# Turned weights at four places modulo 512, and four sequences of the six terms of h

## Chip, cores and metric

The kernel runs on one core of one Trainium2 chip. The metric is the device time of one execution in microseconds. Before the change three runs gave 657.39 us as their median (657.28 to 657.51).

## What is computed

Two attention steps and a gated feed-forward layer, in float32:

```python
p_packed = sm_attn(p, k, v)                 # 32 packed rows per head
out = sm_attn(q, p_packed, p_packed)        # batch 8, heads 8, 576 tokens, 64 wide
x = out.transpose(0, 2, 1, 3).reshape(4608, 512)
h = x @ w_in                                # 512 -> 2048
g = h * sigmoid(1.702 * h)
return g @ w_out                            # 2048 -> 512
```

## The kernel before, in words

The 2048 inner columns are walked in two phases (`ph` 0 and 1), and in each phase in four units `u` of two chunks of 128 columns. A pair of chunks with its rows of `w_out` has the number kp = 4 ph + u; "the four inner chunks" of the change are the four u. For each batch b (0 to 7) and each half (288 of 576 tokens) a unit does this:

- `h_mm` (line 714, matmul at L725) makes h for the unit's two chunks. The second attention step is folded in: the stationary operand is a 128x128 piece of `m` (the packed values times w_in), the moving operand is a row of `a` (the attention weights), 288 columns. Both are split into an upper and a lower float32r part, so that one chunk takes six matmuls into one bank: (even/odd head `eo`, part of m, part of a) = term 0 (0, upper, upper), 1 (0, lower, upper), 2 (1, upper, upper), 3 (1, lower, upper), 4 (0, upper, lower), 5 (1, upper, lower). All units take them in the order 0 to 5. There are 16 halves x 16 chunks x 6 = 1536 of them.
- ScalarE applies the gate (`g_main` L745, `g_over` L751), VectorE forms seven sums of quarters (`g_sum` L795), and both split them into upper and lower parts (`g_upper`, L126; `g_lower` L815): the tile `gs`.
- `prod` (L902) multiplies by w_out after Strassen's scheme with seven products (the "turned weights": sums and differences of quarters of w_out, upper and lower parts, in the tiles `Wa` with four blocks and `Wb` with three). Each product takes three matmuls, upper x upper, upper x lower, lower x upper: stationary a 128x128 piece of `gs`, moving 256 columns of `Wa` or `Wb`. There are 128 unit-halves (2 phases x 16 halves x 4 units); 116 go this way, and 16 more that gather the tokens left over by each half (tiles named `over`): 132 x 7 products x 3 = 2772 matmuls. The other 12 unit-halves, of batch 0, use `prod0` (L842): 12 matmuls each of 512 columns.

Four accumulator banks A to D and two pairs of banks for h hold the results. `a_lower` (L691, VectorE) writes the lower part of `a` for a half, `m_lower` (L597, VectorE) that of `m` for two units; `a_upper` is a copy (L126 on ScalarE, or L128 on VectorE).

The order of all work on every engine is written out by hand, as a list of some thousand steps at the end of the kernel, and each engine runs its own in that order; waits are set by what an instruction reads and writes. A wait stands on the first matmul that reads the late operand, and all later matmuls stand behind it, since TensorE runs them in order.

SBUF places: `places` (line 81) reserves all tiles once, in the order of the table, each slot rounded up to 32 bytes per partition. Tiles `a`, `m` and `gs` stand before the part that the change touches and start at 192 modulo 512 bytes. The weights Wa0 to Wb3 stand behind five small tags (mx1, nb1, sm1, again, mx2), which take 448 bytes together, so that all eight start at 128 modulo 512; their blocks are 1024 bytes long, so every moving operand of `prod` starts at 128 modulo 512. Every stationary operand of `prod` and of `h_mm` starts at 192. The moving operands of h start at 192 (terms 0 and 1), 320 (2 and 3), 448 (4) and 64 (5).

Of the kernel before, what the change touches and what calls it, by code (L numbers as in the profile page):

```python
# [21 lines left out]
def kernel(  # L22
# [41 lines left out]
    G = S // NPK  # L64
    FC = 512
    HC = FC // 2
# [17 lines left out]
        ("a", 2 * S, ABUFS), ("aT", KC * 2 * P, 1), ("X", 8 * P, XBUFS), ("r", 7 * HC, 2),  # L84
        ("pn", 2 * D, 1), ("PT", P, 8), ("raw", 2 * FC, RBUFS), ("over0", 2 * NM, 1),
        ("over1", 2 * NM, 1), ("over2", 2 * NM, 1), ("over3", 2 * NM, 1), ("mx1", 2, 2),
        ("nb1", 2, 2), ("sm1", 2, 2), ("again", 1, 2), ("mx2", G, 2), ("Wa0", 8 * HC, 1),
        ("Wb0", 6 * HC, 1), ("Wa1", 8 * HC, 1), ("Wb1", 6 * HC, 1), ("Wa2", 8 * HC, 1),
        ("Wb2", 6 * HC, 1), ("Wa3", 8 * HC, 1), ("Wb3", 6 * HC, 1), ("rs1", 1, 4), ("rsa", 1, 2),
        ("sm2", G, 2), ("rs2", G, 2),  # L90
    )
    for tag, words, bufs in places:
        for i in range(bufs):
# [24 lines left out]
    def pair_bank(name):  # L118
        return ps_h.tile([P, 2, FC], F32, tag="psh", name=name)
# [588 lines left out]
    def over_tile(ph, g, u):  # L708
        if (ph, g, u) not in over_g:
            over_g[ph, g, u] = wk.tile([P, 2, NM], F32, tag=f"over{u}", name=f"over_{ph}_{g}_{u}")  # L710
        return over_g[ph, g, u]

    def h_mm(ph, b, half, u, i, ap_=None):
        if i == 0 and not ap_:
            st["h", ph, b, half, u] = pair_bank(f"h_{ph}_{b}_{half}_{u}")
        h = st["h", ph, b, half, u][:, i, :NH]
        f = 2 * NU * ph + 2 * u + i
        m, a = st["m", b, f // CF], st["a", ph, b, half]
        at = slice(f % CF * P, (f % CF + 1) * P)
        terms = [(eo, part, 0) for eo in range(2) for part in range(2)]  # L720
        terms += [(eo, 0, 1) for eo in range(2)]
        for n, (eo, part, ap) in enumerate(terms):
            if ap_ not in (None, ap):
                continue
            nc.tensor.matmul(  # L725
                h, m[:, part, eo, at], a[:, ap, eo * NH : (eo + 1) * NH],
                start=(n == 0), stop=(n == len(terms) - 1), skip_group_check=ap_ is not None,
            )
# [229 lines left out]
    def store(b, half, r=None, block=None, engine=nc.sync):  # L958
# [43 lines left out]
        (a_lower_copy, 0, 0, 0, 0), (warm, 7, 1, "D"), (a_lower_mm, 0, 0, 0, 1),  # L1002
        (begin_w, "out", 2, 0, None), (load_w, "in", 0, 1, 1), (max2, 0, 1),
        (h_mm, 0, 0, 0, 0, 0, 0), (a_lower_copy, 0, 0, 0, 1), (load_w, "in", 0, 2, 1),
        (wa_upper, 0, 2, 4), (h_mm, 0, 0, 0, 0, 1, 0), (join_w, "out", 2, 0, None),
        (begin_w, "out", 3, 0, None), (wa_lower_mm, 0, 1), (load_w, "in", 1, 0, None), (sub2, 0, 1),
        (begin_w, "in", 0, 0, 1), (join_w, "out", 3, 0, None), (h_mm, 0, 0, 0, 0, 0, 1),
        (exp2, 0, 1), (table, "gelu"), (h_mm, 0, 0, 0, 0, 1, 1), (join_w, "in", 0, 0, 1),
        (wa_lower_mm, 0, 0), (load_w, "in", 1, 1, None), (g_main, 0, 0, 0, 0, 0), (sum2, 0, 1),
# [830 lines left out]
```

## Time and profile before

| what | value |
|---|---|
| median of three runs | 657.39 us |
| the profiled execution, its own time | 657.49 us |
| span of its instructions | 655.7 us |
| TensorE matmul busy | 647.9 us, 99% of the span |
| VectorE busy | 558.0 us, 85% |
| ScalarE busy | 410.4 us, 63% |
| mean granted TensorE clock | 1.000 |

The span runs from the first to the last instruction; 1.8 us of the execution lie around it. Matmuls are pipelined: one is shown as lasting some 280 to 295 ns while the next starts 113 to 134 ns after it, so busy time says little about how fast they follow each other. That is read from the chain of waits: a piece of it gives the time from the start of a run of matmuls to the start of what follows, and its count; the quotient is the spacing.

### The profile page before, as it was taken

How to read it: one execution, taken by the hardware profiler on the slowest of the kernel's cores; microseconds unless marked ns; L12 is line 12 of the kernel's file. 1: busy time of each engine (PE TensorE's matmuls, PEld its weight loads, DVE VectorE, ACT ScalarE, POOL GpSimd, SP SyncE). 2: the span in 40 equal slices, each digit the busy share in tenths (PEclk: the TensorE clock that was granted, in tenths of full speed). 3: DMA queues.
4: the chain of work that ended last, by engine and by line, in shares of the span. 5: the costliest groups of instructions: out<-in, count | busy, mean ns of one | idle time of the engine just before them, and what ended most of it. 6: DMA issues, size and time to landing. Idle time of an engine off the chain costs nothing.

```text
span 655.7 us, 15348 instructions
## 1 busy us (share of the span) xinstructions
PE 647.9 (99%) x6263; PEld 593.7 (91%) x6263; DVE 558.0 (85%) x1151; ACT 410.4 (63%) x772; POOL 5.4 (1%) x15
## 2 busy tenths in 40 slices
PE   7999999999999999999999999999999999999997
PEld 5777898989989899898999799999999999999997
DVE  3978989789898997978898787977889887978897
ACT  5976977778685886966768755444444463444441
POOL 1100000000000000000000000000000000000000
PEclk9999999999999999999999999999999999999999
DMA  9866565673856737465476341333232423332342
GB/s 336 298 220 236 187 165 204 174 279 73 227 208 162 267 56 298 172 166 178 150 261 186 124 179 65 111 89 121 82 116 88 127 88 89 107 103 75 90 133 109
DMA packets 59318, 104.92 MB, mean 160 GB/s; under 512 B 31408, under 2 KB 36272, under 8 KB 58352
## 3 DMA queue, kind: packets, MB, share of 16 engines
q1 hardware_dynamic: 59104, 103.81, 48.5%
q8 instruction: 49, 0.80, 0.5%
q14 instruction: 21, 0.17, 0.1%
q10 hardware_dynamic: 144, 0.13, 0.1%
HBM read 70.51 MB, written 33.42 MB: 159 GB/s over the span
## 4 chain that ended last, share of the span: by engine, by line
PE 94%; DMA 3%; ACT 1%; SPq 1%; DVE 0%; issue 0%; ACTq 0%
PE h L725 30%; PE accC L902 13%; PE accB L902 13%; PE accA L902 13%; PE accD L902 6%; PE psm_None L573 4%; PE accB L842 2%; PE accB_over L902 2%; PE accA_over L902 2%; PE accC_over L902 2%; PE accA L842 2%; DMA home_m<-w_in 1%; DMA home<-w_in 1%; PE ps L617 1%; PE accD L521 1%; PE ps L310 1%
## 5 line engine op out<-in xcount | busy, mean ns | idle before, releaser
L725 PE MATMUL h<-a,m 128*128 128x288 f32 x1536 | 226.2, 294 | 0.0
L725 PEld LDWEIGHTS h<-a,m 128*128 128x128 f32 x1536 | 208.8, 188 | 2.0 <-ACT gs L126 0.8
L815 DVE TENSOR_TENSOR gs<-X,gs 128x896 fp32r<-128x896 f32 x116 | 125.2, 1087 | 29.8 <-ACT gs L126 29.2
L126 ACT CAST gs<-X 128x896 fp32r<-128x896 f32 (+2 forms) x118 | 106.4, 909 | 62.7 <-DVE X L795 46.1
L795 DVE TENSOR_TENSOR X<-X 128x256 f32<-128x256 f32 (+1 forms) x348 | 108.5, 331 | 20.8 <-ACT X L745 17.3
L745 ACT ACTIVATE X<-h 128x512 f32<-128x512 f32 (+1 forms) x129 | 76.3, 595 | 70.3 <-PE h L725 33.2
L902 PE MATMUL accC<-Wa,gs 128*128 128x256 f32 x696 | 98.4, 281 | 0.0
L902 PE MATMUL accB<-Wb,gs 128*128 128x256 f32 x696 | 97.7, 281 | 0.0
L902 PEld LDWEIGHTS accB<-Wb,gs 128*128 128x128 f32 x696 | 88.3, 189 | 6.0 <-issue 3.4
L902 PEld LDWEIGHTS accC<-Wa,gs 128*128 128x128 f32 x696 | 88.6, 189 | 5.4 <-issue 4.7
L902 PE MATMUL accA<-Wa,gs 128*128 128x256 f32 x348 | 60.3, 282 | 0.0
L902 PE MATMUL accA<-Wb,gs 128*128 128x256 f32 x348 | 59.3, 279 | 0.0
L902 PE MATMUL accD<-Wa,gs 128*128 128x256 f32 x348 | 57.2, 281 | 0.0
L751 ACT ACTIVATE over<-h 128x64 f32<-128x64 f32 x128 | 35.2, 287 | 32.5 <-PE h L725 32.2
L902 PEld LDWEIGHTS accA<-Wa,gs 128*128 128x128 f32 x348 | 49.4, 189 | 2.4 <-issue 2.1
L902 PEld LDWEIGHTS accD<-Wa,gs 128*128 128x128 f32 x348 | 48.1, 189 | 2.6 <-issue 2.6
L902 PEld LDWEIGHTS accA<-Wb,gs 128*128 128x128 f32 x348 | 48.9, 189 | 0.0
L597 DVE TENSOR_TENSOR m<-psm_None,m 128x1024 fp32r<-128x1024 f32 x31 | 37.7, 1217 | 2.2 <-ACT m L126 2.2
L126 ACT CAST m<-psm_None 128x1024 fp32r<-128x1024 f32 x31 | 30.8, 1016 | 10.2 <-PE psm_None L573 10.0
L573 PE MATMUL psm_None<-w_in,PT 64*32 64x512 f32 x496 | 32.2, 596 | 0.1
L691 DVE TENSOR_TENSOR a<-xt,a 128x576 fp32r<-128x576 f32 x31 | 23.2, 749 | 3.2 <-ACT a L126 3.1
L126 ACT CAST a<-xt 128x576 fp32r<-128x576 f32 (+1 forms) x30 | 19.7, 660 | 5.2 <-DVE xt L671 5.2
(208 smaller groups left out, 774.6 us busy)
## 6 DMA issues: line engine op xcount, KB each, us to landing
part<-r SPq DMA_DIRECT2D x14, 896.0 KB, 6.8
p<-part SPq DMA_DIRECT2D x14, 896.0 KB, 5.4
q<-q SPq DMA_DIRECT2D x16, 576.0 KB, 6.1
o<-r SPq DMA_DIRECT2D x16, 512.0 KB, 6.3
raw_out_None<-w_out SPq DMA_DIRECT2D x16, 511.8 KB, 4.0
v<-v SPq DMA_DIRECT2D x7, 1024.0 KB, 6.7
raw_in_None<-w_in SPq DMA_DIRECT2D x12, 511.8 KB, 5.6
k<-pk SPq DMA_DIRECT2D x8, 640.0 KB, 3.9
```

The source lines that it names most:

```text
L126: nc.scalar.copy(dst, src)
L310: nc.tensor.matmul(bank[32 * j : 32 * j + 32, :NH], kq["p", b][rows(eo), j, :], kq["k", b][rows(eo), half, j, :], start=True, stop=True,)
L573: nc.tensor.matmul(banks[eo][32 * j : 32 * j + 32], PT[rows(eo), j, :], w_in_sb[c % 2][rows(eo), j, at], start=True, stop=True,)
L597: nc.vector.tensor_tensor(m[:, 1, :, at], st["bank", "m", b, c, part], m[:, 0, :, at].bitcast(F32), op=ALU.subtract,)
L691: engine.tensor_tensor(even_odd(a[:, 1], eo), even_odd(st["t", 2, b, half], eo), even_odd(a[:, 0], eo).bitcast(F32), op=ALU.subtract,)
L725: nc.tensor.matmul(h, m[:, part, eo, at], a[:, ap, eo * NH : (eo + 1) * NH], start=(n == 0), stop=(n == len(terms) - 1), skip_group_check= ...
L745: nc.scalar.activation(X[:, :4].rearrange("p (f t) n -> p f (t n)", f=2)[:, chunks(f)], st["h", *k][:, chunks(f), :NM], AF.Gelu_apprx_sigm ...
L751: nc.scalar.activation(over_part(ph, b, half, u), st["h", ph, b, half, u][:, :, NM:NH], AF.Gelu_apprx_sigmoid, scale=2.0,)
L795: engine.tensor_tensor(to, a, b_, op=ALU.subtract)
L815: engine.tensor_tensor(lo, X, hi.bitcast(F32), op=ALU.subtract)
L842: nc.tensor.matmul(accs[name], gs[:, gp, 2 * f + r], W[:, wp, 2 * f : 2 * f + 2].rearrange("p n e -> p (n e)"), start=(u == 0 and f == 0 a ...
L902: nc.tensor.matmul(acc[:, n * HC : (n + 1) * HC], gs[:, gp, g], st["W", kp, "ab"[w // 4]][:, wp, w % 4], start=(u == 0 and n == 0 and i == 0),
```

## The change

The small tags are set between the weights, so that each unit's Wa and Wb move together: unit 0 stays at 128 modulo 512, unit 1 starts at 256, unit 2 at 384, unit 3 at 0. No size changes, and all tiles in the table ahead of mx1 stay where they were. Then `h_mm` takes the six terms in a sequence given by the unit: unit 0 as before, unit 1 begins with the two terms that read the lower part of `a`, unit 2 has the terms in the sequence 0, 2, 4, 5, 1, 3, unit 3 goes backwards. The flags that open and close a sum go with the place in the sequence, not with the term. The first half of batch 0 (called with `ap_`) keeps its order where it names a part.

```diff
@@ places @@
-        ("nb1", 2, 2), ("sm1", 2, 2), ("again", 1, 2), ("mx2", G, 2), ("Wa0", 8 * HC, 1),
-        ("Wb0", 6 * HC, 1), ("Wa1", 8 * HC, 1), ("Wb1", 6 * HC, 1), ("Wa2", 8 * HC, 1),
-        ("Wb2", 6 * HC, 1), ("Wa3", 8 * HC, 1), ("Wb3", 6 * HC, 1), ("rs1", 1, 4), ("rsa", 1, 2),
-        ("sm2", G, 2), ("rs2", G, 2),
+        ("Wa1", 8 * HC, 1), ("Wb1", 6 * HC, 1), ("nb1", 2, 2), ("sm1", 2, 2), ("Wa2", 8 * HC, 1),
+        ("Wb2", 6 * HC, 1), ("rs1", 1, 4), ("Wa3", 8 * HC, 1), ("Wb3", 6 * HC, 1), ("again", 1, 2),
+        ("rsa", 1, 2), ("Wa0", 8 * HC, 1), ("Wb0", 6 * HC, 1), ("mx2", G, 2), ("sm2", G, 2),
+        ("rs2", G, 2),
@@ ahead of h_mm, and in it @@
+    turns = ((0, 1, 2, 3, 4, 5), (4, 5, 0, 1, 2, 3), (0, 2, 4, 5, 1, 3), (5, 4, 3, 2, 1, 0))
+
     def h_mm(ph, b, half, u, i, ap_=None):
...
         terms += [(eo, 0, 1) for eo in range(2)]
+        if ap_ is None:
+            terms = [terms[n] for n in turns[u]]
         for n, (eo, part, ap) in enumerate(terms):
```

The order of steps on every engine is the same before and after; what moves are the waits inside h. The two places that follow are on TensorE, in phase 0, where unit 1 is the first to use a half's `a`. In the names, the phase is left out: h_2_0_1 is batch 2, half 0, unit 1.

TensorE, batch 2, half 0, before:

```order
L902 MATMUL accC_1_1_1513<-Wa_728,gs_1_1_2_1494 128x256 x6
L725 MATMUL h_2_0_1_1575<-a_2_0_1538,m_0_1499 128x288 [waits DVE_49,Activation_49]
L725 MATMUL h_2_0_1_1575<-a_2_0_1538,m_0_1499 128x288 x3
L725 MATMUL h_2_0_1_1575<-a_2_0_1538,m_0_1499 128x288 [waits DVE_49]
L725 MATMUL h_2_0_1_1575<-a_2_0_1538,m_0_1499 128x288 x7
```

The same place after the change:

```order
L906 MATMUL accC_1_1_1513<-Wa_728,gs_1_1_2_1494 128x256 x6
L729 MATMUL h_2_0_1_1575<-a_2_0_1538,m_0_1499 128x288 [waits DVE_49]
L729 MATMUL h_2_0_1_1575<-a_2_0_1538,m_0_1499 128x288
L729 MATMUL h_2_0_1_1575<-a_2_0_1538,m_0_1499 128x288 [waits Activation_49]
L729 MATMUL h_2_0_1_1575<-a_2_0_1538,m_0_1499 128x288 x9
```

The wait for VectorE's lower part of `a` stood on the fifth matmul and now stands on the first.

TensorE, batch 3, half 1, before:

```order
L725 MATMUL h_3_1_1_2296<-a_3_1_2269,m_0_2089 128x288 [waits DVE_49,PE_49,Activation_49]
L725 MATMUL h_3_1_1_2296<-a_3_1_2269,m_0_2089 128x288 x3
L725 MATMUL h_3_1_1_2296<-a_3_1_2269,m_0_2089 128x288 [waits DVE_49]
L725 MATMUL h_3_1_1_2296<-a_3_1_2269,m_0_2089 128x288
L902 MATMUL accA_2_1_2071<-Wa_890,gs_2_1_3_2154 128x256 x3
```

The same place after the change:

```order
L729 MATMUL h_3_1_1_2296<-a_3_1_2269,m_0_2089 128x288 [waits DVE_49,PE_49,Activation_49]
L729 MATMUL h_3_1_1_2296<-a_3_1_2269,m_0_2089 128x288 x5
L906 MATMUL accA_2_1_2071<-Wa_890,gs_2_1_3_2154 128x256 x3
L906 MATMUL accA_2_1_2071<-Wb_1220,gs_2_1_3_2154 128x256 x3
L729 MATMUL h_3_1_1_2296<-a_3_1_2269,m_0_2089 128x288 x6
```

Here too the separate wait on the fifth matmul has gone into the first.

## Rows read from the trace of the kernel before

**Rows 1.** The page: busy time by engine, the granted clock in 40 slices, the chain by engine.

```profile
PE 647.9 (99%) x6263; PEld 593.7 (91%) x6263; DVE 558.0 (85%) x1151; ACT 410.4 (63%) x772; POOL 5.4 (1%) x15
...
PEclk9999999999999999999999999999999999999999
...
PE 94%; DMA 3%; ACT 1%; SPq 1%; DVE 0%; issue 0%; ACTq 0%
```

**Rows 2.** The page's costliest groups: TensorE's h and products (count after the x).

```profile
L725 PE MATMUL h<-a,m 128*128 128x288 f32 x1536 | 226.2, 294 | 0.0
...
L902 PE MATMUL accC<-Wa,gs 128*128 128x256 f32 x696 | 98.4, 281 | 0.0
L902 PE MATMUL accB<-Wb,gs 128*128 128x256 f32 x696 | 97.7, 281 | 0.0
...
L902 PE MATMUL accA<-Wa,gs 128*128 128x256 f32 x348 | 60.3, 282 | 0.0
L902 PE MATMUL accA<-Wb,gs 128*128 128x256 f32 x348 | 59.3, 279 | 0.0
L902 PE MATMUL accD<-Wa,gs 128*128 128x256 f32 x348 | 57.2, 281 | 0.0
```

**Rows 3.** The chain, runs of products: start us, us, what, count.

```profile
83.25 1.36 PE accA L902 x12
...
200.69 2.04 PE accB_over L902 x18
...
394.90 2.12 PE accB L902 x18
...
427.99 2.04 PE accB L902 x18
...
648.08 1.41 PE accC_over L902 x12
...
650.55 1.43 PE accC_over L902 x12
```

**Rows 4.** The chain, runs of h, same columns.

```profile
31.91 4.84 PE h L725 x36
47.40 3.16 PE h L725 x24
...
188.87 3.12 PE h L725 x24
...
370.46 3.16 PE h L725 x24
...
546.97 3.90 PE h L725 x30
```

**Rows 5.** The timeline around three first uses of a half's a, TensorE and VectorE.

```profile
107.47 0.74 DVE L691 TENSOR_TENSOR a<-xt,a 128x576 fp32r<-128x576 f32 x1
...
107.87 3.38 PE L725 MATMUL h<-a,m 128*128 128x288 f32 x24
```

**Rows 6.** The same, batch 3, half 1.

```profile
156.11 1.77 PE L725 MATMUL h<-a,m 128*128 128x288 f32 x12
...
156.53 0.76 DVE L691 TENSOR_TENSOR a<-xt,a 128x576 fp32r<-128x576 f32 x1
```

**Rows 7.** The same, batch 7, half 0.

```profile
307.88 0.76 DVE L691 TENSOR_TENSOR a<-xt,a 128x576 fp32r<-128x576 f32 x1
...
308.91 1.75 PE L725 MATMUL h<-a,m 128*128 128x288 f32 x12
```

## The prediction

> **What bounds the kernel.** I read the page first, then the chain of waits, then the timeline at the places where a wait moves. The page shows TensorE's matmuls busy for 647.9 of 655.7 us, and the chain that ended last runs through TensorE for 94% of the span; VectorE has 15% and ScalarE 37% of the span free. The granted clock is full in every slice [rows 1]. So TensorE is the bound from end to end, each nanosecond between two of its matmuls counts, and nothing that the change does elsewhere matters unless TensorE has to wait for it. The change adds no instruction to any engine and removes none: only addresses and the sequence inside h differ. What can move is therefore how fast matmuls follow each other, and where TensorE stands still.
>
> The profile's durations (281 ns for a product, 294 for h [rows 2]) overlap. The spacing is the length of a piece of the chain divided by its count, and it isn't one number. Products of one shape, with operands at the same places modulo 512, run at 1.36 / 12 = 113.3 ns in one stretch and at 2.12 / 18 = 117.8 ns in another; 2.04 / 18 = 113.3 and 1.41 / 12 = 117.5 are further ones [rows 3]. Of the 55 runs of 12 or 18 products that the chain lists (the first and the last are the first and last of rows 3), I count 20 at 113.3 to 115 ns, 31 at 117.5 to 117.8 and 4 above. h has more such speeds: 3.12 / 24 = 130.0 ns and 3.90 / 30 = 130.0; 3.16 / 24 = 131.7; 4.84 / 36 = 134.4 [rows 4]. Of 72 runs of 12 and more, 20 are at 130.0, 36 at 131.2 to 132.2 and 16 above. A run keeps its spacing over many matmuls, through several accumulators and whatever the other engines do. I take this for two or three regular rhythms between a moving operand that is read and the next weights that are loaded meanwhile: TensorE falls into one, and stays until something breaks it. That is a reading, no row shows the cause.
>
> **The change part by part.** *The waits.* Unit 1 now begins with the two terms that read the lower part of `a`. In most halves that part is ready in time: in batch 7, half 0, VectorE ends at 307.88 + 0.76 = 308.64 us and h of unit 1 starts at 308.91 [rows 7], so nothing is added. In two halves it isn't. Batch 2, half 0: VectorE ends at 107.47 + 0.74 = 108.21, h starts at 107.87 [rows 5]: 0.34 us of standing still, where the fifth matmul at 107.87 + 4 x 0.132 = 108.40 found it ready before. Batch 3, half 1: the merged row from 156.11 holds six matmuls of unit 3 and six of this h, which therefore starts near 156.11 + 6 x 0.132 = 156.90; VectorE ends at 156.53 + 0.76 = 157.29 [rows 6]: 0.39 us. Behind the waiting matmul stands all of TensorE's work, and those who wait for h (ScalarE's gate, then VectorE's sums) start as much later; they have slack, so the loss is TensorE's alone. Nobody gives it back later, since TensorE hardly waits afterwards. Together 0.73 us, with a little for the hand-over **0.8 us**. Units 2 and 3 come behind units 0 and 1 in these halves, and the lower part of `m` is read later than before in units 1 and 2; I cost them at nothing. If a half came to start with unit 3, it would pay as unit 1 does.
>
> *The places of the weights.* Units 1 to 3 are three quarters of 2,772 products (696 + 696 + 3 x 348 = 2,436 [rows 2], and 336 for the left-over tokens): 2,079 matmuls whose moving operand now starts at another place against the stationary one. No row shows a product at another place, so I bound it by the two rhythms. The mean over both is (20 x 113.5 + 31 x 117.6) / 51 = 116.0 ns. All at 113.3: 2,079 x -2.7 = **-5.6 us**. All at 117.6: 2,079 x 1.6 = **+3.3 us**. The nearest row on places is h, whose six terms have four different places of the moving operand against the same place of the stationary one, and whose mean spacing in a given rhythm is still 130.0 or 131.7 [rows 4]: a mixture of places gives no fast or slow extreme. And since both rhythms of the products occur at one and the same place [rows 3], the place alone doesn't choose the rhythm. I therefore take **0**, the mixture as it is, and keep both ends for the range.
>
> The Trainium skill says, in "TensorE: Matmul & The Clock Gate", Part 2, step 1, that TensorE has two independent read ports into SBUF, one for the moving operand and one for the weights, and that loading the next weights takes no bandwidth from the running matmul. By that rule alone the places would be worth nothing whatever they are, and 0.8 us of waits would be all. The two spacings at one shape [rows 3] say that something beside the column count does set the pace, so I let the rule speak for my zero without taking the bounds away.
>
> *The sequence of h.* Unit 0 is unchanged, and unit 1 is the same cycle begun elsewhere: over two chunks in a row the same operand follows the same operand. Units 2 and 3 are new: half of 1,536 matmuls [rows 2], 768. Mean now about 131.9 ns. All at 130.0: 768 x -1.9 = -1.5 us; all at 134.4, the slowest steady run: 768 x 2.5 = +1.9 us [rows 4]. I take 0, nearest to the commonest speed, 131.7. The 144 matmuls of `prod0` are too few to matter: 2 ns each would be 0.3 us.
>
> **The sum.** 657.4 + 0.8 + 0 + 0 = **658.2 us**. The profiled execution took 657.49 us, 655.7 of them span; the median of the runs is 657.39, so both stand within 0.1 us, and I add to the median. About 0.2%, or 1.3 us, is what a measurement of this kernel can tell from no change: the forecast lies inside.
>
> **The rivals.**
>
> *A, the forecast:* the rhythms mix as before. If the fast share among the changed products moves by 20 points either way, that is 2,079 x 0.2 x 4.3 = 1.8 us: 656.4 to 660.0. For it: rows 3, one place, both rhythms. Against: unit changes now change the place as well, so that runs through several units may break more often. Chance 0.42. Of this 0.26 lies within 0.2%, 0.14 above, 0.02 below.
>
> *B, faster:* at the new places the fast rhythm catches more often, as the moving operand is further from the weights that are loaded. 658.2 - 5.6 - 1.5 = 651.1 at most; half of it is 654.6. For it: 113.3 ns is reached and held over 18 products [rows 3]. Against: nothing in the rows ties it to a distance. Chance 0.28.
>
> *C, slower:* the new places lock into the slow rhythm. Place: the products of units 1 to 3, and h of units 2 and 3. Price: up to 3.3 + 1.9, so 658.2 + 5.2 = 663.4; half is 660.8. It decides against A once the fast share among the changed products is under about a quarter. For it: the slow rhythm is the commoner one already, 31 runs of 51, and it is there at the end of the kernel too (1.41 / 12 at 648.08 [rows 3]). Against: as for B. Chance 0.30.
>
> That the change doesn't do what it says can be left out for the places, which follow from the table's sizes; for the sequences, the moved waits show it in the order.
>
> **How the numbers follow.** Faster by over 0.2%: 0.28 + 0.02 = 0.30. Within: 0.26. Slower: 0.30 + 0.14 = 0.44. The range leaves out the outermost tenth on each side: B's better third (under 652.5) and C's worse third (over 662.5). A's own range is 656.4 to 660.0.
>
> **What would show it.** In the profile after: TensorE stands still for 0.3 to 0.4 us ahead of h in batch 2, half 0, and batch 3, half 1, with VectorE's `a` as the releaser; if it doesn't, the waits were mis-read. The chain's runs of products in units 1 to 3 should still show 113.3 and 117.5 ns, in a mixture near two to three; runs of unit 0 serve as the control. A third speed that unit 1, 2 or 3 keeps to itself would mean that the place does choose, and the sum would go by that unit's 693 products times the difference. In h, units 2 and 3 should lie between 130 and 134 ns; under 130 or over 135 the bounds are wrong. A total outside 652.5 to 662.5 means that one of these speeds isn't among those seen before.

## The result: 661.16 us, slower by 0.55%

The changed kernel takes 661.16 us (median of four runs, 660.83 to 661.35) against 657.45 us before: a ratio of 1.0055, with a 95% interval of 1.0043 to 1.0066, 3.7 us. It is inside the range forecast and on the side that had the largest chance, but above the 660.0 us at which the likeliest case ended. In some executions, of most of the kernels here, TensorE's granted clock is at its lower level for a while near the start (0.50, or 1.2 GHz, from 11 to 14 us in the trace of `e3_all192`), and they are 1 to 2 us longer; of the medians below this bears on that of `e10_change_a64`.

The page of the kernel after: matmul busy time, the granted clock, TensorE's largest group.

```profile
span 659.0 us, 15347 instructions
...
PE 651.0 (99%) x6263; PEld 596.7 (91%) x6263; DVE 558.0 (85%) x1151; ACT 410.5 (62%) x772; POOL 5.4 (1%) x15
...
PEclk9999999999999999999999999999999999999999
...
L729 PE MATMUL h<-a,m 128*128 128x288 f32 x1536 | 227.8, 295 | 0.4 <-DVE a L691 0.3
```

Against [rows 1] and [rows 2], nothing has changed but TensorE: 651.0 us of matmuls instead of 647.9, over a span that is 3.3 us longer, with VectorE and ScalarE where they were and the clock full. Two things are to be told apart in these 3.3 us: standing still, and spacing.

**Standing still.** The timeline after, around the first use of a half's `a` in batch 2, half 0, and in batch 3, half 1 (in brackets what ended the idle time):

```profile
107.25 0.73 DVE L691 TENSOR_TENSOR a<-xt,a 128x576 fp32r<-128x576 f32 x1
...
108.04 3.07 PEld L729 LDWEIGHTS h<-a,m 128*128 128x128 f32 x23 [0.31 <-DVE a L691]
...
156.91 0.76 DVE L691 TENSOR_TENSOR a<-xt,a 128x576 fp32r<-128x576 f32 x1
...
157.81 1.03 PE L729 MATMUL h<-a,m 128*128 128x288 f32 x6 [0.31 <-DVE a L691]
```

At both places TensorE now waits 0.31 us for VectorE's lower part of `a` (at the first the row is that of the weight load, PEld), where it began at once before [rows 5, 6]. That is idle time, counted from the end that the profile models for the matmul ahead. From start to start the two places lose more. In batch 2, half 0, the last product and the first h take 389 and 237 ns, against 113 and 131 elsewhere; in batch 3, half 1, the last h of unit 3 and the first of unit 1 take 602 and 207 ns, against 131 and 132. That is 0.38 and 0.55 us, 0.93 together.

**Spacing.** One stretch, batch 6, half 1, TensorE alone, shows the products. By the order written in the kernel these are accB unit 0; accC units 0 and 1; accA unit 0 (Wa, then Wb); accB unit 1; accD units 0 and 1; accA unit 1. The timeline of the kernel before:

```profile
304.83 1.52 PE L902 MATMUL accC<-Wa,gs 128*128 128x256 f32 x12
306.19 0.50 PE L902 MATMUL accA<-Wa,gs 128*128 128x256 f32 x3
306.53 0.50 PE L902 MATMUL accA<-Wb,gs 128*128 128x256 f32 x3
306.87 0.84 PE L902 MATMUL accB<-Wb,gs 128*128 128x256 f32 x6
307.55 0.84 PE L902 MATMUL accD<-Wa,gs 128*128 128x256 f32 x6
308.23 0.50 PE L902 MATMUL accA<-Wa,gs 128*128 128x256 f32 x3
308.57 0.50 PE L902 MATMUL accA<-Wb,gs 128*128 128x256 f32 x3
```

The same stretch after:

```profile
306.75 1.58 PE L906 MATMUL accC<-Wa,gs 128*128 128x256 f32 x12
308.16 0.51 PE L906 MATMUL accA<-Wa,gs 128*128 128x256 f32 x3
308.51 0.50 PE L906 MATMUL accA<-Wb,gs 128*128 128x256 f32 x3
308.85 0.87 PE L906 MATMUL accB<-Wb,gs 128*128 128x256 f32 x6
309.56 0.86 PE L906 MATMUL accD<-Wa,gs 128*128 128x256 f32 x6
310.25 0.52 PE L906 MATMUL accA<-Wa,gs 128*128 128x256 f32 x3
310.61 0.51 PE L906 MATMUL accA<-Wb,gs 128*128 128x256 f32 x3
```

Start to start, before: 0.68 / 6 = 113.3 ns in unit 0 and unit 1 alike. After: unit 0's accA takes 0.35 and 0.34 us for three (117 and 113 ns), unit 1's accB 0.71 / 6 = 118.3 and its accA 0.36 / 3 = 120. One stretch could be chance. So I took from the trace, for all products and all h, the mean time from one start to the next; gaps over 160 ns, which are restarts behind other work, are left out. The unit follows from the order. The sums are those of all gaps up to the start of whatever matmul follows, restarts and waits included.

| kernel | products, mean ns by unit 0, 1, 2, 3 | sum, us | h, mean ns by unit | sum, us |
|---|---|---|---|---|
| before | 116.3, 116.2, 116.1, 116.4 | 328.7 | 131.6, 131.7, 131.5, 131.8 | 203.7 |
| after | 115.8, 117.6, 116.2, 117.8 | 330.7 | 132.3, 132.9, 132.6, 132.4 | 205.6 |

Units 1 and 3 pay 1.0 us each in their products, unit 2 0.3; unit 0 gains 0.4. Unit 2's 0.3 is no spacing: it is the part of the first wait that falls on the gap behind its last product. h takes 1.9 us more, of which 0.65 are the rest of the two waits. Together 3.8 us: 1.6 of spacing in the products, 1.3 in h, 0.9 of waits. The twelve unit-halves with 512 columns give back 0.3 and the rest of TensorE 0.2, which leaves the 3.3 us of the span. In units 1 and 3 the rhythm of 113.3 ns is nearly gone. Of all threes of products on one operand, from the first start to the start of what follows and with the restarts left out, 6% and 3% run at 114 ns or less, against 34% and 28% before; units 0 and 2 have 38% and 27%, against 28% and 35%. This is one execution of each kernel, and the totals of one kernel differ by about 1 us from run to run, so that a smaller difference between two traces shows little by itself.

### The profile page after: what moved, and what is told of

Same layout as the page of the kernel before. It is cut to its first block, busy times and chain, and to the rows that moved or that the text cites. A ratio compares the mean times of both kernels' runs of the same rounds, so it can differ in the third digit from the quotient of the medians.

```text
span 659.0 us, 15347 instructions
## 1 busy us (share of the span) xinstructions
PE 651.0 (99%) x6263; PEld 596.7 (91%) x6263; DVE 558.0 (85%) x1151; ACT 410.5 (62%) x772; POOL 5.4 (1%) x15
## 4 chain that ended last, share of the span: by engine, by line
PE 93%; ACT 3%; DVE 3%; DMA 1%; issue 0%; SPq 0%; DVEq 0%
PE h L729 30%; PE accA L906 12%; PE accC L906 12%; PE accB L906 12%; PE accD L906 6%; PE psm_None L573 4%; PE accB L846 2%; PE accB_over L906 2%; PE accA_over L906 2%; PE accC_over L906 2%; PE accA L846 2%; PE ps L617 1%; PE accD L521 1%; PE ps L310 1%; PE accD_over L906 1%; PE accC L846 1%
```

## The experiments

Three theories went in. **P:** the distance in bytes from the moving weights to the stationary piece chooses the rhythm, and it counts modulo 256: units 1 and 3, which come to 448 and 192 modulo 512, are both 192 modulo 256, units 0 and 2 (64 and 320) both 64. **T:** the places are innocent, and the new sequences of h spoil what follows them. **W:** the moved waits cost what they show. **E** came later: what a sequence of h leaves behind chooses the rhythm of the products behind it. All twelve kernels are the kernel before, or the changed one, with the edit that is shown, timed against the kernel before on the same chip.

### One half of the change at a time, and one distance for all

`e1_places`: the table of the change, h as before.

```diff
...
-        if ap_ is None:
-            terms = [terms[n] for n in turns[u]]
```

> The weights at the four places of the change, the terms of h in the order of before. Theory P (the place of the moving weights against the stationary piece, counted modulo 256 bytes, chooses the rhythm of the products): units 1 and 3, whose distance from weights to stationary piece is 192 modulo 256, run at 117.5 to 118 ns almost throughout, units 0 and 2 (distance 64) mix 113.3 and 117.7 as before; products cost about 2.0 us more, the 512-wide products of units 1 and 3 about 0.3 us less, the total is near 659.2 us. Rival T (the places are innocent, the new sequences of h spoil the rhythms, those of the products behind them too): 657.4 us, units 1 and 3 as before.

Measured: 659.81 us, ratio 1.0038 (1.0026 to 1.0051). The chain of `e1_places`, the run that answers to the one at 200.69 us of [rows 3], units 1 to 3:

```profile
200.68 2.12 PE accB_over L902 x18
```

It starts within 0.01 us of its old time and runs at 2.12 / 18 = 117.8 ns instead of 113.3.

`e2_turns`: the sequences of the change, the table of before.

```diff
-        ("Wa1", 8 * HC, 1), ("Wb1", 6 * HC, 1), ("nb1", 2, 2), ("sm1", 2, 2), ("Wa2", 8 * HC, 1),
...
+        ("nb1", 2, 2), ("sm1", 2, 2), ("again", 1, 2), ("mx2", G, 2), ("Wa0", 8 * HC, 1),
...
```

> The weights where they were before, the terms of h in the four sequences of the change. Theory P: the products keep the mixture of before in all four units (mean near 116.2 ns); the sequences cost what they cost inside h, 0.7 us of waiting in two halves and about 1 ns on each matmul of units 1 to 3 (1.0 us): near 659 us. Rival T: the products of units 1 and 3 go slow here too, total near 661 us.

Measured: 657.63 us, ratio 1.0005 (0.9996 to 1.0013).

`e3_all192` and `e4_all320`: only small tags move, so that 320 or 192 bytes of them stand ahead of all weights.

```diff
-        ("nb1", 2, 2), ("sm1", 2, 2), ("again", 1, 2), ("mx2", G, 2), ("Wa0", 8 * HC, 1),
+        ("mx1", 2, 2),
+        ("nb1", 2, 2),
+        ("mx2", G, 2),
+        ("Wa0", 8 * HC, 1), ("Wb0", 6 * HC, 1),
...
```

In `e4_all320` mx2 alone stands there:

```diff
-        ("nb1", 2, 2), ("sm1", 2, 2), ("again", 1, 2), ("mx2", G, 2), ("Wa0", 8 * HC, 1),
+        ("mx2", G, 2),
+        ("Wa0", 8 * HC, 1), ("Wb0", 6 * HC, 1),
...
```

> All eight weights at 0 modulo 512, so that every product has the distance that unit 3 has in the change (192), h in the order of before. Theory P: all four units at 117.7 ns almost throughout, products 4 us more than before, 512-wide ones 229 instead of 233 ns (0.6 us less): 660.5 to 661 us. Rival T: 657.4 us.

> All eight weights at 384 modulo 512, the distance of unit 2 in the change (320), h in the order of before. Theory P with a period of 256 bytes: the same distance as before modulo 256, so the same mixture, and 657.4 us, within 0.5. Rival with a period of 512 bytes: each distance has a mixture of its own, and this one, seen in unit 2 alone, need not be that of before; a difference of over 1 us either way would speak for it. Rival T: 657.4 us.

Measured: `e3_all192` 660.19 us, ratio 1.0041 (1.0027 to 1.0055); `e4_all320` 656.80 us, ratio 0.9996 (0.9987 to 1.0005).

| kernel | products, mean ns by unit | sum, us | h, mean ns by unit | sum, us |
|---|---|---|---|---|
| e1, places alone | 116.2, 118.0, 116.2, 118.0 | 331.1 | 131.8, 131.7, 131.8, 131.9 | 203.9 |
| e2, sequences alone | 115.4, 115.2, 115.4, 115.5 | 327.1 | 132.0, 132.7, 132.8, 132.2 | 205.4 |
| e3, all at 192 | 117.0, 117.1, 117.2, 117.3 | 331.2 | 131.9, 131.8, 132.0, 131.9 | 204.1 |
| e4, all at 320 | 116.1, 115.8, 115.7, 116.0 | 327.8 | 131.9, 131.6, 131.6, 132.0 | 203.8 |

The chain of `e3_all192`, two runs of 18 products, which answer to the runs at 200.69 and 427.99 us of [rows 3]:

```profile
202.52 2.12 PE accB_over L911 x18
...
430.65 2.12 PE accB L911 x18
```

Both ran at 2.04 / 18 = 113.3 ns before and run at 117.8 now, with the same work in the same order ahead of them. In `e1_places` the change of unit shows within one run, the one that answers to 427.99 us: its threes follow each other at 118.0 and 117.0 ns in unit 1, 114.7 and 115.0 in unit 2, 117.7 and 117.3 in unit 3, where all six stand at 113.3 to 113.7 before. So the places do it, and T falls: it had `e1_places` at no loss and `e2_turns` at 661 us. P holds in its main point: distance 192 modulo 256 holds the slow rhythm (99% of the threes or more at 117 ns and above in units 1 and 3 of `e1_places`; 82 to 88% in `e3_all192`, less than expected), and 320 is like 64 within 0.5 ns and within the error of the total. But P was wrong on `e2_turns`: it had the products untouched there. They gain 1.6 us, since 54 to 60% of the threes run at 114 ns or less, and this pays for the 1.8 us that h loses. The halves don't add up (1.0038 and 1.0005 against 1.0055), though the ratios alone, with their intervals, don't tell that from chance. The traces do: the sequences speed the products up by 0.7 to 1.0 ns (by unit) at the old places, but by 0.4, 0.4, 0.0 and 0.2 ns at the new ones, while their cost inside h stays. Units 1 and 3 can hardly take the fast rhythm there; why units 0 and 2 lose most of the gain too, no run shows.

One thing stays untested here and below. In every run the stationary pieces of the products start at 192 modulo 512, and only the weights move. So a distance between the two operands and a place of the moving operand by itself (128 modulo 256 where the distance is 64) fit all these runs alike. Where the text says distance, either may be meant.

### Other distances

`e5_probe`: four distances that hadn't been seen, one for each unit, set by small tags and a pad of 32 bytes.

```diff
+        ("Wa0", 8 * HC, 1), ("Wb0", 6 * HC, 1),
+        ("rs1", 1, 4),
+        ("Wa1", 8 * HC, 1), ("Wb1", 6 * HC, 1),
+        ("pad", 8, 1),
+        ("Wa2", 8 * HC, 1), ("Wb2", 6 * HC, 1),
+        ("mx1", 2, 2),
+        ("Wa3", 8 * HC, 1), ("Wb3", 6 * HC, 1),
...
```

> The terms of h in the order of before; weights of the four units at distances from weights to stationary piece that modulo 256 are 0 (unit 0), 128 (unit 1), 96 (unit 2) and 32 (unit 3), none of which has been seen. Theory P says only that each unit keeps a mixture of its own, that repeats over the batches, between 113.3 and 118 ns on average, so that the units differ by over 0.5 ns; 64 gave 116, 192 gave 117 to 118. If the distance acts as a smooth shift, 32 and 96 lie near 64 and 0 and 128 between 64 and 192. Rival (only the half of the 256 bytes counts, over or under 128): 0, 32, 96 as 64 and 128 as 192. Total 657 to 660 us.

Measured: 664.17 us, ratio 1.0113 (1.0100 to 1.0127). Products by unit 118.8 (distance 0), 118.6 (128), 118.1 (96), 118.4 ns (32). The chain of `e5_probe`, the same two runs:

```profile
202.96 2.14 PE accB_over L912 x18
...
432.95 2.12 PE accB L912 x18
```

No three products run at 114 ns anywhere. Both readings offered fall: 32 and 96 aren't near 64, 0 and 128 don't lie between 64 and 192, and 0 and 32 aren't like 64. P's own bounds fell as well: its units were to average 113.3 to 118 ns and the total to be 657 to 660 us. Of the six distances modulo 256 that were tried, 64 alone reaches 113.3 ns often; each of these four was tried in one unit of one kernel.

### The waits

`e6_unit1_back` and `e12_change_u1_back`: unit 1 takes its terms as before; in the first at the weights' old places, in the second in the changed kernel.

```diff
-    turns = ((0, 1, 2, 3, 4, 5), (4, 5, 0, 1, 2, 3), (0, 2, 4, 5, 1, 3), (5, 4, 3, 2, 1, 0))
+    turns = ((0, 1, 2, 3, 4, 5), (0, 1, 2, 3, 4, 5), (0, 2, 4, 5, 1, 3), (5, 4, 3, 2, 1, 0))
```

> The weights where they were before, the sequences of the change, but unit 1 in the order of before. Theory W (the waits moved to the head of unit 1 cost 0.7 to 0.8 us): TensorE doesn't stand still ahead of unit 1 in batch 2, half 0, and batch 3, half 1; h of unit 1 drops from 132.7 to near 131.7 ns (0.4 us); 656.5 us if the products keep the faster mixture they had with all four sequences (mean 115.4), 657.5 if that mixture came from unit 1's sequence. Rival (the stalls are made up for later): no change against all four sequences, 657.6.

> The change as it is, but unit 1 in the order of before, so that the waits for the lower part of a stand on the fifth matmul again. Theory W: 0.65 us of standing still ahead of unit 1 in two halves goes, and about 0.4 us of slower h of unit 1; 1.0 us less than the change, near 660.2 us. Rival (those waits are taken back later): no more than 0.4 us less, 660.8.

Measured: `e6_unit1_back` 656.39 us, ratio 0.9993 (0.9984 to 1.0002), against 1.0005 with all four sequences; `e12_change_u1_back` 659.85 us, ratio 1.0042 (1.0027 to 1.0056), against 1.0055 for the change. Each step is 0.12 to 0.13%, 0.8 us; the intervals overlap, so the size rests on the traces. There the wait for `a` is gone, h of unit 1 is at 131.9 and 131.7 ns, h in all takes 0.9 and 1.1 us less, and the products stay at 115.2 to 115.5 ns in `e6_unit1_back`: the better mixture doesn't come from unit 1. W holds as far as this goes: the totals fall by about what the traces show of the waits, so that no sign is seen of the stalls being made up for later.

### What chooses the rhythm behind h

`e7_a64`: a small tag of 64 bytes ahead of `a`, taken from ahead of the weights, which stay; the tiles between `a` and the weights move with `a`, but none of them is an operand of h or of the products.

```diff
-        ("a", 2 * S, ABUFS), ("aT", KC * 2 * P, 1), ("X", 8 * P, XBUFS), ("r", 7 * HC, 2),
+        ("mx1", 2, 2), ("a", 2 * S, ABUFS), ("aT", KC * 2 * P, 1), ("X", 8 * P, XBUFS), ("r", 7 * HC, 2),
...
-        ("over1", 2 * NM, 1), ("over2", 2 * NM, 1), ("over3", 2 * NM, 1), ("mx1", 2, 2),
+        ("over1", 2 * NM, 1), ("over2", 2 * NM, 1), ("over3", 2 * NM, 1),
```

> The order and the weights' places of before, but the tiles of a (and those behind them, the weights excepted) 64 bytes further, so that the distances of h, which were 0 and 128 modulo 256, become 192 and 64. Theory P: the rhythm is a matter of the distance between moving and stationary operand in h as well: its mean leaves 131.7 ns by over 0.3 ns, the pattern over its six terms is another, and the products' mixture changes with what comes ahead of them; total off 657.5 by over 1 us, either way. Rival (distances matter for the products alone): h as before, 657.5.

`e8_all_u2`: one sequence for all units, at the weights' old places.

```diff
-    turns = ((0, 1, 2, 3, 4, 5), (4, 5, 0, 1, 2, 3), (0, 2, 4, 5, 1, 3), (5, 4, 3, 2, 1, 0))
+    turns = ((0, 2, 4, 5, 1, 3),) * 4
```

> The weights where they were before, all four units with the sequence that unit 2 has in the change (0, 2, 4, 5, 1, 3). Theory E (what the sequence of h leaves behind chooses the rhythm of the products after it): the share of products at 113.3 ns differs from the 35% of before and from the 55% of the four sequences together, in all units alike; if this sequence is the one that feeds the fast rhythm, over 60%, and 656.5 us with h at 132.8 ns and 0.1 us of waits; if not, 658.5. Rival (the better mixture came from changing sequences from unit to unit): the share stays near 35%, 658.5 to 659 us.

`e9_a64_u2` has both edits, `e10_change_a64` is the changed kernel with that of `e7_a64`, `e11_a32` moves `a` by 32 bytes (a pad of 8 words ahead of it, and one in the place of a small tag behind it, so that the weights stay).

> The weights where they were before, a 64 bytes further, and all units with the sequence 0, 2, 4, 5, 1, 3: the two edits that each raised the share of products at 113.3 ns (to about 65 to 70%). Theory E (what h leaves behind chooses the rhythm): they act through the same thing, so that the gains don't add; a share over 65% and 655 to 656 us. Rival (independent gains): over 85% at 113.3 ns, 654 us.

> The change as it is, with a 64 bytes further. Theory P (the distance 192 modulo 256 locks the products of units 1 and 3 into the slow rhythm, whatever comes ahead of them): units 1 and 3 stay at 117.5 to 118 ns, units 0 and 2 rise to the faster mixture (near 114.5 ns); 659.5 us. Rival (the rhythm of h decides and the place only shifts the odds): units 1 and 3 come to under 116.5 ns too, 657.5 us.

> The order and the weights' places of before, a 32 bytes further: the distances of h become 224 and 96 modulo 256. If a 32-byte step acts on h as it did on the products (all three such distances ran at 118 to 119 ns, slower than 64 and 192), h leaves 131.8 ns upwards, 133 to 135, and the total is 657.5 to 660 us; if h is governed by the 64-byte lines alone, it is as before or as with 64 bytes, 655.5 to 657.5 us.

| kernel | us | ratio (95% interval) | products, mean ns by unit | sum, us | h, mean ns by unit | sum, us |
|---|---|---|---|---|---|---|
| e7_a64 | 655.49 | 0.9977 (0.9968 to 0.9986) | 114.5, 114.4, 114.5, 114.6 | 324.3 | 133.2, 133.2, 133.1, 133.1 | 206.0 |
| e8_all_u2 | 656.49 | 0.9997 (0.9988 to 1.0006) | 115.2, 114.7, 114.8, 114.7 | 325.3 | 132.7, 132.9, 132.8, 132.8 | 205.7 |
| e9_a64_u2 | 654.32 | 0.9954 (0.9942 to 0.9965) | 114.4, 114.3, 114.3, 114.3 | 324.1 | 132.3, 132.3, 132.2, 132.2 | 205.2 |
| e10_change_a64 | 661.23 | 1.0058 (1.0043 to 1.0073) | 115.6, 117.7, 115.1, 117.8 | 329.9 | 133.1, 132.8, 132.1, 132.1 | 205.6 |
| e11_a32 | 657.44 | 1.0006 (0.9998 to 1.0015) | 115.8, 115.3, 115.1, 115.3 | 327.0 | 133.1, 133.0, 132.9, 133.0 | 205.7 |

The chain of `e8_all_u2`, the run that answers to the one at 394.90 us of [rows 3]:

```profile
395.73 2.04 PE accB L906 x18
```

The chain of `e9_a64_u2`, the run that answers to the one at 394.90 us of [rows 3], the run behind it, and h where [rows 4] has 546.97:

```profile
393.68 2.04 PE accB L906 x18
...
426.66 2.04 PE accB L906 x18
...
544.88 3.97 PE h L729 x30
```

The first ran at 2.12 / 18 = 117.8 ns before, its weights and its `gs` at the same places; it runs at 113.3 in both kernels. What has changed ahead of it is h: its sequence, and in `e9_a64_u2` the place of its moving operand as well. E holds: what runs ahead of the products sends them into one rhythm or the other where the place allows both. Its rival for `e8_all_u2`, the change from unit to unit, falls: one sequence for all does better than four (65 to 75% of the threes at 114 ns or less). Where an edit of h speeds the products up, h itself gets slower (3.97 / 30 = 132.3 ns here, 130.0 before), and the gain is the difference. The two edits of `e9_a64_u2` don't add up on the products (324.1 us against 324.3 with `e7_a64` alone, 66 to 75% of the threes at 114 ns or less against 65 to 71%); its further gain by the traces is 0.7 us in h. Its total, 654.32 us, is near the rival's 654 and under E's 655 to 656; what speaks for E is the share, which the rival had at over 85%. `e10_change_a64` is the test of the lock: units 1 and 3 stay at 117.7 to 117.8 ns whatever h leaves, as P said. But units 0 and 2 came to 115.6 and 115.1 ns, not to 114.5, and the total didn't fall to the 659.5 us that P expected. Its six runs are two groups of three, 660.2 to 660.4 and 662.1 to 662.3 us, and its median stands between them; the first group is 0.8 to 0.9 us under the 661.16 of the change, 0.25 of it with the kernel before (657.20 us there, on another chip, against 657.45), and its products take 0.8 us less than the change's (329.9 against 330.7). `e11_a32` came out at 657.44 us, where the two expectations meet (657.5), and decides neither: h rose as it did with 64 bytes, and the products gained about as much as h lost.

`e9_a64_u2`, at 0.9954, beats the kernel before and the changed one. Its page beside [rows 1], 3.0 us less of span:

```profile
span 652.7 us, 15348 instructions
...
PE 645.6 (99%) x6263; PEld 590.2 (90%) x6263; DVE 557.4 (85%) x1151; ACT 410.2 (63%) x772; POOL 5.4 (1%) x15
```

## Why the prediction was right, and where it wasn't

**What bounds the kernel:** right. Nothing but TensorE's spacing and its stops shows in the difference.

**The waits:** right in mechanism and place, and near in size. 0.34 and 0.39 us were forecast, 0.8 with the hand-over; from start to start 0.38 and 0.55 us were lost, 0.93 together. The part of it that is more than idle time, the slow restart behind the wait, was underrated. That nobody gives it back is what `e12_change_u1_back` agrees with.

**The places, taken at 0:** this is the step that failed. It read "since both rhythms of the products occur at one and the same place, the place alone doesn't choose the rhythm". Place 64 allows both, and all the rows of before were at that place; 192 holds one. Two rhythms at one place don't speak for the same two at another. The other support was h, in which four places mix and which shows no extreme: its distances are 0 and 128 modulo 256, and with neither had a product been seen. Where it was tried (`e5_probe`), products at those two ran at 118.6 to 118.8 ns, above the bound of 117.6 that I had put as the slow end. For the change's own places the end about held: units 1 and 3 came to 117.6 and 117.8 ns.

The Trainium skill states ("TensorE: Matmul & The Clock Gate", Part 2, step 1) that loading the next weights takes nothing from the running matmul's read bandwidth, and this was let speak for the zero. The runs differ from what was drawn from it: with only the weights and some small tags moved, products of unit 1 average 116.2 ns (`before`), 117.1 (`e3_all192`) and 118.6 (`e5_probe`), so the measurement decides. That the two reads disturb each other is a reading that fits; no run here shows that they do.

**The sequence of h, taken at 0:** the bound was right (-1.5 to +1.9 us for two units), the middle wasn't. All four units slowed, by 0.6 to 1.2 ns, 1.3 us without the waits; unit 1, which I had called the same cycle begun elsewhere, by 1.2, and unit 0, whose sequence hadn't changed, by 0.7. So h, too, depends on what comes ahead of it. What I missed altogether is that the sequences act on the products behind them: -1.6 us at the old places.

**The rivals:** case C's place (products of units 1 to 3) was right in two units of three, its time, 660.8 us at half its price, near the 661.16 measured. Case A was given the larger chance on the strength of the step that failed. The control that was named, unit 0 against the others, is what showed it.

**The number:** of the 3.7 us, the sum held 0.8, for the waits; the rest are the two terms put at 0. The range took the result in because its bounds came from the two rhythms, on behalf of a case that was thought less likely. That half of C's price lies within 0.4 us of the result is luck: it priced the products of three units and h of two, and the products of two units, h of four and the waits paid.

## To carry to other kernels

When TensorE is busy from end to end with matmuls that each load new weights, as here, the place of the moving operand against the stationary one is a tuning parameter: a few small tiles moved around in SBUF were worth from -0.2% to +1.1% here, at no cost. One run can try a distance per unit, but their effects are tied to what runs ahead, so an edit that helps one group of matmuls has to be judged by the sum of all. And an operand that is read first makes its writer's lateness show: moving late terms to the head of a sum cost 0.4 and 0.55 us at the two places where the writer had finished just in time.

## What was not expected of the hardware

- Products of 128x128 by 256 columns run for long stretches at either 113.3 or 117.8 ns, and at one place of the weights keep the one they are in through changes of accumulator and operand. Of the six distances modulo 256 tried, 64 allows both, 192 mostly the slow one (0 to 17% of the threes at 114 ns or less, by kernel and unit), and 0, 32, 96 and 128 average 118.1 to 118.8 ns with no three under 115.
- The preferences aren't the same for other lengths. Products of 512 columns average 229.2 to 231.7 ns at distance 192 and 232.8 to 233.8 at 64 (`before`, the change, `e1_places`, `e3_all192`). h, with 288 columns, has no place that is better by itself: in the sequence of before it is slower at 64 and 192 (133.2 ns, `e7_a64`) than at 0 and 128 (131.7), in the sequence 0, 2, 4, 5, 1, 3 it is faster there (132.2 ns, `e9_a64_u2`, against 132.8, `e8_all_u2`).
- The order in which six matmuls of one sum are issued, with the same operands and the same count, changed the share of fast threes of products behind them from 28 to 35% (by unit) to 65 to 75% (`e8_all_u2`).
- Why 256 bytes, why a rhythm lasts, and whether it is the distance or the moving operand's own place that counts, stays open: no run here looks into it.
